# Half-size products for one more batch, and another order of the last stores, in an attention and mixer kernel

## The chip, the cores and the metric

The kernel runs on one core of a Trainium2 chip. The metric is the time of one execution on the device in microseconds (us), and less is better. Several runs of one kernel are summed up by their median. A profile is one further execution, taken by the hardware profiler: it gives the start and the length of each instruction on each engine. The engines are TensorE (PE in the profile; its weight loads are listed apart as PEld), VectorE (DVE), ScalarE (ACT), GpSimd (POOL) and SyncE (SP), which here only issues DMAs. Each engine works through its own queue in order, and an instruction that has to wait holds up all that stand behind it on that engine.

## The reference: what is computed

Four batches, each of 8 heads, 768 positions and a head width of 64, go through an attention with a window of 128 and 4 sink positions. Its output (768 x 512 for each batch) goes through a mixer: one product pair over the positions (768 to 256 to 768), and then one over the channels (512 to 1536 to 512), each with a ReLU between.

```python
scores = scale * np.matmul(q, k.transpose(0, 1, 3, 2))
rel = pos[:, None] - pos[None, :]
keep = (pos[None, :] < n_sink) | ((rel >= 0) & (rel < window))
a = softmax(np.where(keep, scores, -1e9))        # exp over its sum + 1e-9
x = np.matmul(a, v)                              # heads side by side: 4 x 768 x 512
h = np.maximum(x.transpose(0, 2, 1) @ w_tok1, 0.0) @ w_tok2
u = x + h.transpose(0, 2, 1)
h2 = np.maximum(u @ w_ch1, 0.0) @ w_ch2          # w_ch1 512 x 1536, w_ch2 1536 x 512
out = u + h2
```

The change lies in the last product, `relu(u @ w_ch1) @ w_ch2`, and in how its result is added to u and stored. Here the batches are called first to fourth; in the code they are b = 0 to 3.

## The kernel before

All is bf16 on TensorE with fp32 sums in PSUM. PSUM has eight banks: four single ones, `ps_ga` to `ps_gd`, which everything but the scores uses in turn, and two pairs, `ps_sa` and `ps_sb`, for the scores. Once the last score has been computed, the pairs serve the products too.

The work is written as small tasks: a function that issues instructions, an engine or a choice of engines, an estimated duration, the tasks that it depends on, and a priority. `Plan.order` plays these tasks through with the estimated durations, picks for each engine the ready task of lowest priority, chooses the PSUM bank, and so fixes the order in which each engine's instructions are issued. At the end the priorities are overwritten by the table `RANK`, one number for each task in the order of their making. So the order on all engines is decided before the run; on the chip, only the waits between engines are left. The order is one interleaving of the attention of a later batch with the mixer of an earlier one.

The stages of the mixer, for batch b:

- `make_tok`: the product pair over positions (the lines L999 and L1041 of the profile), then `u = h + x` on DVE (L1047) and a DMA transpose of u into `uT` (L1053), issued from SP.
- `ch1(half, ft)` in `make_channel` (L1100): 24 groups of four matmuls over 384 columns, one for each half of the positions and each of 12 channel tiles. Each fills one bank, and a ReLU on ACT (L1058) or DVE (L1060) moves it to `v1`, which holds `[channel, position]`.
- the product with `w_ch2`. The first two batches do it by `ch2` (L1249): six position tiles, each 12 matmuls over 512 columns into one bank, in three parts of four. The result is added to u by one DVE instruction of 512 columns (L1265) and stored by one DMA of 256 KB (L1280).
- The third and the fourth batch do it by `products` (L1151): v1 is split into quarters a11, a12, a21, a22 by position and channel, w_ch2 likewise, and seven products of half size take the place of eight. `sub` (L1126) makes four sums of quarters on DVE, in three chunks of 768 elements each: S3 = a11 - a21, S1 = a21 + a22, S2 = S1 - a11, S4 = a12 - S2. They lie in the tiles that the profile names x_ba or x_bb (S3), q32a (S1), k32a (S2) and v (S4). The tiles q32a and k32a are the landing place of the q and k loads of even groups of heads, so a sum has to wait until POOL has cast what was loaded there. `make_weight_sums` (L1076) makes the four sums of quarters of w_ch2 once, as eight DVE or POOL instructions.

A product is one task: six matmuls of 256 columns. `pair(i)` combines the products of the position tiles i and i + 3 into their output tiles by `read` (L1182, L1184, and L1179 for the one that adds one product to both halves of a tile), always on DVE. The sequence `TURNS`, a list of product number and pair, gives the first order of the products, before `RANK`. The products 1, 6 and 7 of a pair follow each other in one bank, with a read after each; products 5 and 3 share another.

In the last pair of the last batch, before the change, the first output tile stores its left half, the second tile its whole width, and product 3 closes: in two pieces of 128 columns, each read and stored by itself (L1227), the very last from ACT's queue.

Of the kernel before, what the change touches and what calls it, by code (L numbers as in the profile page):

```python
# [44 lines left out]
ACT_MORE = 0.05  # L45
LATE_CAST = [None, None, ('ACT', 'DVE'), ('ACT', 'DVE'), ('ACT', 'DVE')]
MASK_ENG = {0: ('DVE',), 1: ('POOL',), 2: ('POOL',), 3: ('POOL',), 4: ('POOL', 'DVE'), 5: ('DVE',), 6: ('POOL', 'DVE'), 7: ('POOL',)}
KS_ENG = {0: ('POOL', 'ACT'), 1: ('ACT', 'DVE'), 2: ('ACT', 'DVE'), 3: ('POOL', 'DVE'), 4: ('ACT', 'DVE'), 5: ('ACT', 'DVE'), 6: ('ACT',
    'DVE'), 7: ('ACT', 'DVE')}
# [7 lines left out]
RANK = [0, 0, 27, 389, 474, 75, 75, 0, 0, 50, 50, 110, 130, 410, 150, 1105, 74, 556, 294, 761, 901, 1005, 1169, 1384, 1534, 2175, 2603,  # L57
    3040, 3395, 2965, 3530, 100, 170, 520, 570, 170, 1751, 1345, 1564, 1613, 1352, 2093, 3275, 3682, 350, 249, 319, 310, 319, 461, 424,
    691, 663, -90, -209, 525, 525, 1010, 704, 830, 510, 587, 609, 844, 971, 1062, 1305, 1485, 406, 731, -132, 783, 711, 1347, 963, 1080,
    504, 1220, 1285, 1341, 1431, 1332, 1606, 1681, 2305, 2886, 2489, 1812, 1948, 2034, 1968, 1353, 1432, 2116, 2138, 2764, 2198, 2143,  # L60
    2171, 2307, 831, 963, 909, 1267, 142, 1053, 1318, 1371, 1354, 1867, 1194, 1489, 1520, 1191, 1717, 1365, 1590, 1782, 1644, 1468,
    1884, 1751, 2006, 1825, 1636, 1968, 2208, 1979, 2328, 1501, 1921, 1829, 2331, 1924, 1941, 2257, 2251, 2726, 2394, 2424, 2250, 2394,
    2507, 2285, 2344, 2470, 2240, 2466, 2385, 2482, 2421, 3095, 2898, 2330, 2692, 2563, 2706, 2589, 2651, 2773, 3162, 2922, 3261, 3351,
    2965, 2635, 2984, 3084, 2930, 2521, 3370, 3380, 3033, 3404, 3353, 3213, 3889, 3385, 3694, 3110, 3509, 3495, 3414, 3640, 3729, 5285,
    3724, 3740, 3659, 4045, 3754, 3810, 3479, 3735, 4001, 4476, 3986, 4082, 4091, 4307, 4123, 3669, 4098, 3974, 4055, 4201, 4100, 4586,
    4475, 4501, 4510, 5226, 4622, 4848, 4627, 4623, 4542, 4898, 4917, 5099, 5128, 5244, 5246, 5391, 5293, 5496, 6289, 5519, 5924, 5949,
    6243, 6486, 6575, 6044, 6899, 6655, 6790, 6910, 7063, 7112, 7523, 7555, 7715, 7836, 7169, 7737, 8153, 8173, 8261, 8289, 8553, 8707,
    8835, 8971, 4021, 3787, 4465, 3215, 3969, 4124, 4116, 4190, 3897, 3672, 3524, 3908, 4037, 3989, 4113, 4126, 4506, 4505, 4683, 4692,
    4922, 4362, 5079, 5243, 3683, 5355, 4388, 4009, 5244, 5700, 4483, 5261, 5079, 5363, 5605, 5991, 5620, 5761, 5654, 5741, 5798, 5854,
    4927, 5262, 4827, 5342, 4431, 5086, 4375, 5649, 5329, 5427, 5403, 5237, 5068, 5398, 5523, 5596, 6036, 5743, 5970, 6049, 6037, 6377,  # L70
    6393, 6398, 5703, 5515, 6148, 6326, 6581, 7097, 6834, 6797, 6772, 6806, 6785, 6856, 6779, 6868, 7043, 7106, 7077, 6436, 6036, 6062,
    6041, 6128, 7285, 7091, 7170, 7257, 7349, 7487, 7291, 7402, 8027, 7886, 7664, 7781, 8011, 7874, 7938, 8166, 7967, 8067, 8371, 7940,
    8067, 8376, 8866, 8952, 8301, 9017, 9075, 9161, 9140, 9226, 9217, 9303, 9272, 9368, 9347, 9493, 9500, 9556, 9730, 9786, 10365, 9521,
    9931, 9087, 9966, 10052, 10290, 10396, 10805, 10441, 10420, 10386, 10365, 10451, 10430, 10621, 10792, 10980, 11056, 10636, 10722,
    10787, 10853, 10799, 10965, 10944, 11400, 11209, 11280, 11101, 11419, 11581, 11095, 11241, 11306, 11392, 11458, 11484, 11523, 11539,
    11688, 11360, 11943, 12070, 12114, 11614, 11787, 12109, 12127, 12171, 12076, 12278, 11777, 12564, 12721, 12132, 12473, 12721, 12916,
    13080, 5334, 5349, 5339, 5389, 5449, 5853, 6011, 6070, 5819, 6001, 6186, 6000, 6528, 6663, 6069, 6324, 6602, 7140, 6884, 6904, 6246,
    7229, 6864, 7416, 7434, 7523, 6923, 7024, 7390, 6820, 6953, 7038, 7459, 7746, 7260, 7298, 7822, 8185, 8434, 8235, 8187, 8285, 8242,
    8305, 8217, 8325, 8221, 8405, 5489, 5604, 5679, 5784, 5929, 6024, 6699, 6204, 7103, 6553, 6845, 7306, 7444, 6963, 7432, 8330, 8090,
    8390, 7903, 8534, 8610, 8748, 8847, 8996, 9096, 9123, 9213, 8520, 8803, 8864, 9022, 9229, 9365, 8605, 9273, 9412, 9487, 9436, 9537,  # L80
    9565, 9591, 9570, 9041, 9695, 9811, 8452, 8599, 8548, 8634, 9800, 9916, 9835, 9952, 10031, 10095, 10236, 10074, 10155, 10361, 10747,
    10244, 10506, 10190, 10304, 10641, 10203, 10334, 10736, 10247, 10414, 10801, 7900, 8157, 8490, 8538, 8496, 8573, 8763, 8841, 13190,
    12686, 12808, 12902, 12953, 12429, 13017, 13103, 13074, 13199, 13159, 13245, 13224, 13310, 13289, 13305, 13412, 13498, 13581, 13587,
    13646, 13732, 13842, 13928, 13907, 13993, 14061, 14137, 14086, 14172, 14151, 14237, 14332, 14418, 14671, 15357, 14819, 14805, 14804,
    14890, 14967, 15053, 15367, 15473, 15563, 15329, 15628, 15714, 14187, 14252, 14314, 14096, 15292, 14740, 15396, 15492, 15444, 15559,
    15620, 15718, 14903, 14689, 14968, 15055, 15042, 15816, 15748, 15849, 15177, 15263, 15879, 15965, 15944, 16031, 16089, 16039, 15034,
    15120, 15111, 15203, 15813, 15932, 16141, 16227, 16793, 16879, 16401, 16927, 16924, 17046, 17135, 17035, 15301, 15577, 16206, 16293,
    16616, 16710, 16727, 16814, 16662, 16748, 16858, 16986, 16989, 17079, 17185, 17085, 9191, 9286, 9381, 9566, 9621, 9726, 9721, 9926,
    8307, 10121, 10191, 10475, 10827, 10846, 10956, 12423, 12363, 12425, 12478, 12598, 12695, 12752, 12811, 12968, 13048, 13064, 13455,
    12554, 12655, 12858, 12976, 13246, 13314, 13082, 13149, 13054, 13402, 13377, 13452, 13477, 13543, 13512, 13433, 13547, 13933, 9801,  # L90
    10046, 9541, 10636, 10791, 10786, 11271, 11396, 9511, 11103, 12533, 12703, 13011, 12591, 13099, 13964, 13970, 13972, 14072, 14202,
    14253, 14484, 14605, 14632, 14722, 14832, 14179, 14291, 14427, 15039, 14701, 14987, 14869, 14901, 15032, 15156, 15055, 15126, 15176,
    15232, 15211, 15282, 15246, 15332, 13711, 13798, 13777, 13863, 15282, 15589, 15498, 15434, 15093, 15677, 15831, 15776, 15517, 15956,
    15779, 15877, 16041, 15523, 15936, 16206, 15866, 15996, 16331, 15909, 16056, 16456, 16988, 17426, 17053, 17491, 17718, 17556, 17183,
    17621, 17248, 17686, 17313, 17901, 17228, 17816, 17443, 17881, 17508, 17946, 17573, 18011, 17638, 18076, 17703, 18131, 17848, 18206,
    17833, 18271, 17898, 18336, 17963, 18401, 18114, 18466, 18266, 18531, 18417, 18596, 18442, 18811, 18633, 18988, 18785, 19053, 19236,
    19118, 19001, 19183, 18394, 18469, 18551, 18613, 18684, 18749, 18830, 18881, 20076, 19241, 19322, 19403, 18640, 18767, 18715, 18848,
    19424, 19517, 19358, 19451, 19293, 19484, 19620, 19707, 19555, 19641, 19689, 19781, 18771, 18929, 18836, 18976, 19489, 19576, 19686,
    19772, 20013, 20101, 19751, 20148, 20144, 20268, 20332, 20222, 19082, 19289, 19227, 19370, 19882, 19969, 19948, 20034, 19817, 19903,
    20079, 20208, 19417, 19988, 20282, 20210, 20301, 20382, 20243, 20321, 20355]  # L100
STRASSEN = {2, 3}
EARLY_P = {2: 0, 3: 4}
TURNS = '10 20 11 21 60 50 61 70 30 40 51 12 22 71 42 62 52 41 72 31 32'
S_CHUNK = 2
S_ENG = {1: ('DVE',), 2: ('DVE',), 3: ('DVE',)}
T_ENG = ('POOL', 'DVE')

SEM = 0.05
PE_TAIL = 0.16


def flat_list(x):
    return [z for y in x for z in (flat_list(y) if isinstance(y, (list, tuple)) else [y])]


# [220 lines left out]
def kernel(  # L336
# [742 lines left out]
    def make_channel(b):  # L1079
# [7 lines left out]
        if b == 0 and RES_DMA:  # L1087
            for x in range(2):
                def f(t, x=x):
                    nc.sync.dma_start_transpose(out=u.rearrange("p t d -> p (t d)").rearrange("p (n d) -> p n d", d=P)[:, ts(x, 2 * NT)],  # L1090
                                                in_=uT_[:, 2 * x:2 * x + 2].rearrange("p c s -> p (c s)"))
                M.back.append(add("SP", 1.3, f, [M.turn, L["v3"], L["k3"]], prio=BIAS.get("back", 0) + 5, dma=2.7, run=0.42))
        seq = iter(range(base, base + 200))

        def ch1(half, ft):
            slot = Slot()

# [245 lines left out]
    with tc.manual_schedule():  # L1343
# [3 lines left out]

        for t, r in zip(plan.tasks, RANK):
            t.prio = r
# [38 lines left out]
```

## Time and profile before

| what | value |
|---|---|
| runs (us) | 203.08, 202.29, 203.17, 203.13; median 203.11 |
| profiled execution | 202.05 us, of which the span from the first to the last instruction is 200.3 us |
| mean granted TensorE clock | 0.998 |
| busy in the span: PE | 192.7 us (96%) |
| busy in the span: DVE, ACT, POOL | 125.3 us (63%), 107.2 us (54%), 66.7 us (33%) |
| HBM read, written | 26.77 MB, 6.29 MB |
| PE waits above 0.1 us after the first 20 us | one, of 0.4 us |

The profiled execution is 0.24 us below the fastest and 1.06 us below the median of the four runs. Its own sums are therefore made within its 200.3 us span, and only the difference is carried over to the median.

The columns of a group row are: line, engine, operation, output <- inputs, size, number of instructions; then the busy time, the mean time of one in ns, and the idle time before them. In a row of the timeline they are: start, length, engine, line, operation, and in brackets how long the engine had been idle and what ended it. Matmuls overlap in their pipeline, so the length of one matmul in a group row (380 ns for 512 columns) is longer than the step from one to the next; the chain of waits gives the steps.

### The profile page before, as it was taken

The numbers are of one execution on the slowest core, as the hardware profiler recorded it, in microseconds if no ns is written. First come the engines' busy times: TensorE is split into PE (matmuls) and PEld (weight loads), VectorE is DVE, ScalarE is ACT, GpSimd is POOL, SyncE is SP. The second block draws the span as 40 slices with busy tenths as digits, with TensorE's granted clock in tenths as the row PEclk, the third lists the DMA queues.
The fourth block names the chain that finished last, engine by engine and source line by source line (L and its number), as shares of the span: only waits on it lengthen the run. The fifth ranks groups of instructions, "written<-read, shape, count | busy, mean of one in ns | idle before, by whom it ended". The sixth has DMA issues, their size and how long they took to land.

```text
span 200.3 us, 4471 instructions
## 1 busy us (share of the span) xinstructions
PE 192.7 (96%) x1742; PEld 123.8 (62%) x1742; DVE 125.3 (63%) x303; ACT 107.2 (54%) x188; POOL 66.7 (33%) x110
## 2 busy tenths in 40 slices
PE   7799999999999999999999999999999999999992
PEld 2444876656665655657645544576587687658881
DVE  4689870747655779978262112885699964056782
ACT  2799377788978852496614203787813003773000
POOL 8994422047795762200614011004870000000000
PEclk9999999999999999999999999999999999999999
DMA  5999999999399999699998599900000256100034
GB/s 171 357 229 181 209 206 334 225 266 199 94 285 186 235 188 130 169 150 185 202 197 149 115 203 236 273 12 3 0 0 3 47 165 207 57 0 3 26 146 142
DMA packets 74870, 30.98 MB, mean 155 GB/s; under 512 B 63650, under 2 KB 71202, under 8 KB 74850
## 3 DMA queue, kind: packets, MB, share of 16 engines
q1 hardware_dynamic: 43938, 18.85, 42.4%
q0 software_dynamic: 29680, 10.22, 41.7%
q10 hardware_dynamic: 1232, 1.64, 2.4%
q8 instruction: 13, 0.21, 0.5%
q14 instruction: 7, 0.06, 0.1%
HBM read 26.77 MB, written 6.29 MB: 165 GB/s over the span
## 4 chain that ended last, share of the span: by engine, by line
PE 82%; DMA 11%; DVE 2%; POOL 1%; ACTq 0%; issue 0%; DVEq 0%
PE ps_ga L1100 9%; DMA w_tok<-in_moe_w_tok_dram 8%; PE ps_gc L1100 8%; PE ps_gd L1100 8%; PE ps_gb L1100 7%; PE ps_gb L1249 5%; PE ps_gd L1249 4%; PE ps_gc L1249 4%; DMA k32a<-in_k_dram 3%; PE ps_ga L1151 3%; PE ps_gb L1151 3%; PE ps_ga L1249 3%; PE ps_sa L825 2%; PE ps_sa L1151 2%; PE ps_gc L1151 2%; PE ps_gd L1151 2%
## 5 line engine op out<-in xcount | busy, mean ns | idle before, releaser
L1100 PEld LDWEIGHTS <-w_ch 128*128 128x128 bf16 x384 | 36.7, 98 | 24.4 <-issue 1.4
L1058 ACT ACTIVATE v<-ps_gc 128x384 bf16<-128x384 f32 x22 | 10.8, 492 | 25.7 <-PE ps_gc L1100 25.5
L1249 PEld LDWEIGHTS <-v 128*128 128x128 bf16 x144 | 13.4, 98 | 14.0 <-issue 0.6
L1151 PEld LDWEIGHTS <-v 128*128 128x128 bf16 x150 | 14.1, 98 | 2.3
L1058 ACT ACTIVATE v<-ps_ga 128x384 bf16<-128x384 f32 x21 | 10.4, 494 | 6.8 <-PE ps_ga L1100 6.5
L1058 ACT ACTIVATE v<-ps_gd 128x384 bf16<-128x384 f32 x17 | 8.3, 490 | 8.2 <-PE ps_gd L1100 7.3
L1249 PE MATMUL ps_gb<-w_ch,v 128*128 128x512 bf16 x48 | 12.3, 380 | 0.0
L1100 PE MATMUL ps_ga<-uTa,w_ch 128*128 128x384 bf16 x56 | 11.4, 326 | 0.0
L1100 PE MATMUL ps_gd<-uTa,w_ch 128*128 128x384 bf16 x52 | 10.6, 326 | 0.4 <-DVE x_bb L955 0.4
L479 POOL DMA_DIRECT2D vab<-in_v_dram x4 | 5.7, 1437 | 14.9 <-PE ps_gd L937 12.4
L1100 PE MATMUL ps_gc<-uTb,w_ch 128*128 128x384 bf16 x52 | 10.6, 326 | 0.0
L999 PEld LDWEIGHTS <-w_tok 128*128 128x128 bf16 x96 | 9.1, 98 | 2.0 <-issue 0.4
L1058 ACT ACTIVATE v<-ps_gb 128x384 bf16<-128x384 f32 x17 | 8.4, 492 | 3.6 <-PE ps_gb L1100 3.4
L1100 PE MATMUL ps_ga<-uTb,w_ch 128*128 128x384 bf16 x48 | 9.8, 326 | 0.0
L1249 PE MATMUL ps_gd<-w_ch,v 128*128 128x512 bf16 x36 | 9.2, 379 | 0.0
L1249 PE MATMUL ps_gc<-w_ch,v 128*128 128x512 bf16 x36 | 9.2, 379 | 0.0
L1100 PE MATMUL ps_gb<-uTb,w_ch 128*128 128x384 bf16 x44 | 9.0, 327 | 0.0
L1100 PE MATMUL ps_gc<-uTa,w_ch 128*128 128x384 bf16 x44 | 9.0, 326 | 0.0
L436 POOL CAST kbb<-k32b 128x768 bf16<-128x768 f32 x5 | 4.3, 874 | 13.4 <-DMA k32b<-in_k_dram 13.4
L479 POOL DMA_DIRECT2D vaa<-in_v_dram x4 | 6.0, 1490 | 7.8 <-PE ps_ga L937 6.5
L1100 PE MATMUL ps_gb<-uTa,w_ch 128*128 128x384 bf16 x40 | 8.1, 327 | 0.0
L1100 PE MATMUL ps_gd<-uTb,w_ch 128*128 128x384 bf16 x40 | 8.1, 326 | 0.0
(399 smaller groups left out, 506.3 us busy)
## 6 DMA issues: line engine op xcount, KB each, us to landing
q32a<-in_q_dram SPq DMA_DIRECT2D x4, 384.0 KB, 4.4
vaa<-in_v_dram POOLq DMA_DIRECT2D x4, 384.0 KB, 11.8
vab<-in_v_dram POOLq DMA_DIRECT2D x4, 384.0 KB, 11.9
w_ch<-in_moe_w_ch_dram POOLq DMA_DIRECT2D x3, 512.0 KB, 15.0
w_ch<-in_moe_w_ch_dram POOLq DMA_DIRECT2D x2, 768.0 KB, 19.6
q32b<-in_q_dram SPq DMA_DIRECT2D x8, 192.0 KB, 7.6
k32b<-in_k_dram SPq DMA_DIRECT2D x8, 192.0 KB, 3.5
out_dram<-oa SPq DMA_DIRECT2D x4, 256.0 KB, 4.8
```

The source lines that it names most:

```text
L436: on(t).tensor_copy(out=o, in_=i)
L479: t = add(eng, hold, lambda t: e.dma_start(out=o, in_=i), deps, prio=prio, dma=work, run=run)
L825: nc.tensor.matmul(half(slot, i)[:, at:at + w].rearrange("p (c q) -> p c q", q=P), qkT(kT, g, j)[ds(64 * i, 64), kt], qkT(qT, g, j)[ds(64 ...
L999: nc.tensor.matmul(flat(slot)[:, 0:GH * D], w_tok1[:, n, ts(tt, P)], x[:, n, ds(a * GH * D, GH * D)], start=(n == 0), stop=(n == NT - 1))
L1058: nc.scalar.activation(o, i, AF.Relu)
L1100: nc.tensor.matmul(flat(slot)[:, 0:HS], w_ch1[:, c, ts(ft, P)], uT_[:, c, ds(half * HS, HS)], start=(c == 0), stop=(c == NC - 1))
L1151: nc.tensor.matmul(flat(slot)[:, 0:cw], A[n][0][:, x, ts(i, P)], W[n][:, x, ds(c0, cw)], start=(first and x == 0), stop=(x == NH - 1), ski ...
L1249: nc.tensor.matmul(flat(slot)[:, 0:cw], v1[:, ft, ts(st, P)], w_ch2[:, ft, ds(c0, cw)], start=(ft == 0), stop=(ft == NF - 1 and (b > 0 or ...
```

## The change

1. `STRASSEN` takes in b = 1: the second batch's last product goes by seven half products instead of by `ch2`. The sums of w_ch2 are made before it, that is with the first batch.
2. In the last pair of the last batch, product 3 comes before product 4, and product 4 is the one done in two pieces. The residual of the second tile's left half is copied into its output tile ahead of time by a new copy on ACT or POOL (`keep`), and the wide read of product 7 adds to that. Both tiles are stored by quarters or halves: left and right half of the first, right half of the second, and its left half in two pieces.
3. The engines allowed for the masks of group 6 (`MASK_ENG`, now POOL alone) and for the small copies of sink keys (`KS_ENG`) change, and ACT's surcharge in the planner goes (`ACT_MORE`).
4. `RANK` is a new table, so the order on every engine is another one. `seq2` and the addition of 15000 are part of how priorities are numbered.

```diff
-ACT_MORE = 0.05
+ACT_MORE = 0
-MASK_ENG = {0: ('DVE',), ... 4: ('POOL', 'DVE'), 5: ('DVE',), 6: ('POOL', 'DVE'), 7: ('POOL',)}
-KS_ENG = {0: ('POOL', 'ACT'), 1: ('ACT', 'DVE'), 2: ('ACT', 'DVE'), 3: ('POOL', 'DVE'), 4: ('ACT', 'DVE'), ...
+MASK_ENG = {0: ('DVE',), ... 4: ('POOL', 'DVE'), 5: ('DVE',), 6: ('POOL',), 7: ('POOL',)}
+KS_ENG = {0: ('ACT',), 1: ('POOL', 'ACT', 'DVE'), 2: ('POOL', 'ACT', 'DVE'), 3: ('POOL', 'ACT', 'DVE'), 4: ('ACT', 'DVE'), ...
-RANK = [0, 0, 27, 389, 474, 75, 75, 0, 0, 50, ...
+RANK = [0, 12, 27, 429, 556, 90, 80, 0, 0, 50, ...
-STRASSEN = {2, 3}
-EARLY_P = {2: 0, 3: 4}
-TURNS = '10 20 11 21 60 50 61 70 30 40 51 12 22 71 42 62 52 41 72 31 32'
+STRASSEN = {1, 2, 3}
+EARLY_P = {1: 0, 2: 0, 3: 4}
+TURNS = '10 20 11 21 60 50 61 40 70 51 41 30 12 71 22 62 52 31 72 32 42'
...
+        seq2 = iter(range(base + 30000, base + 30200)) if b == B - 1 else seq
...
                 d = Slot()
-                p4 = product(i, 4, d, True, True, [])
-                r4 = read(o2, d, 0, DH, [p4, w2], op=ALU.subtract, res=s2, frees=True)
                 p7 = product(i, 7, a, False, True, [r6])
-                r7 = read(o2, a, 0, DM, [p7, r4, r5], frees=True, wide=True)
-                order += [(4, p4), (7, p7)]
+                order.append((7, p7))
                 if not end:
+                    p4 = product(i, 4, d, True, True, [])
+                    r4 = read(o2, d, 0, DH, [p4, w2], op=ALU.subtract, res=s2, frees=True)
+                    r7 = read(o2, a, 0, DM, [p7, r4, r5], frees=True, wide=True)
+                    order.append((4, p4))
...
                 else:
                     store(s1, o1, 0, DH, [r2])
                     r5b = read(o1, bb, DH, DH, [p5, r6], frees=True)
-                    store(s2, o2, 0, DM, [r7])
+                    p3 = product(i, 3, d, True, True, [])
+                    r3 = read(o1, d, DH, DH, [p3, r5b], frees=True)
+                    store(s1, o1, DH, DH, [r3])
+                    order.append((3, p3))
+
+                    def keep(t):
+                        copy(t, o2[:, 0:DH], u[:, s2, 0:DH])
+                    r0 = add(("ACT", "POOL"), {"ACT": act(DH, True), "POOL": 0.4}, keep, w2, prio=6)
+                    r7 = read(o2, a, 0, DM, [p7, r0, r5], frees=True, wide=True)
+                    store(s2, o2, DH, DH, [r7])
                     for x in range(2):
                         e = Slot()
-                        p = product(i, 3, e, True, True, [], c0=128 * x, cw=128)
-                        r = read(o1, e, DH + 128 * x, 128, [p, r5b], frees=True)
-                        store(s1, o1, DH + 128 * x, 128, [r], x == 1)
-                        order.append((3, p))
+                        p = product(i, 4, e, True, True, [], c0=128 * x, cw=128)
+                        r = read(o2, e, 128 * x, 128, [p, r7], op=ALU.subtract, frees=True)
+                        store(s2, o2, 128 * x, 128, [r], x == 1)
+                        order.append((4, p))
...
-                    t.prio = M.early_prio + 0.01 * n if n < EARLY_P[b] else next(seq)
+                    t.prio = M.early_prio + 0.01 * n if n < EARLY_P[b] else next(seq2)
...
+        for t in plan.tasks[len(RANK):] if RANK else []:
+            if t.prio < 1000 and t.eng != ("SP",):
+                t.prio += 15000
```

## The prediction

> **What bounds the kernel now.** I read the busy table first, then the busy time by stretches, then PE's waits and the chain of waits, and last the timeline at the places that the change touches.
>
> ```profile
> span 200.3 us, 4471 instructions
> PE 192.7 (96%) x1742; PEld 123.8 (62%) x1742; DVE 125.3 (63%) x303; ACT 107.2 (54%) x188; POOL 66.7 (33%) x110
> ```
>
> ```profile
> 100.00:110.00 10.00, 10.00 (x55) 5.18 (x54) 4.47 (x7) 3.60 (x8) 3.20 (x4) 1.00 1.23 171
> 110.00:120.00 10.00, 10.00 (x51) 4.80 (x49) 1.40 (x3) 1.47 (x3) 0.83 (x1) 1.00 0.76 155
> ...
> 150.00:160.00 10.00, 9.56 (x89) 7.18 (x86) 9.61 (x24) 2.03 (x5) 0.00 (x0) 1.00 0.09 19
> ```
>
> ```profile
> PE ps_gd L1100 <- DVE x_bb L955: 0.4, 1, 0.4
> ```
>
> ```profile
> 102.45 0.86 PE ps_gb L1249 x4
> ...
> 145.89 0.66 PE ps_ga L1151 x6
> ```
>
> In the stretches the columns are length, then PE, PEld, DVE, ACT, POOL, the clock, DMA. PE is full from 20 to 195 us at full clock, but for 0.44 us near 150 us, where it waits for a busy DVE. So PE work removed in between shortens the run one for one, as long as the others keep up. In the second batch's last product (100 to 124 us) DVE is almost idle; in the third batch's (150 to 160 us) DVE is full: that is what seven products cost DVE when attention work runs beside them. The chain gives the steps: four matmuls of 512 columns 0.86 us (215.6 ns each), six of 256 columns 0.656 us (109.3 ns each).
>
> **PE work of the second batch.** Removed: 18 groups of four, 18 x 0.862 = 15.5 us. Added: 21 products, 21 x 0.656 = 13.8 us. All other PE instructions stay in number. Saved: 1.7 us, all on the path. Here a rule speaks against the change: the Trainium skill, TensorE: Matmul & The Clock Gate, Back-to-back issue gap, gives for streams of weight load and matmul a sustained 81 ns at 128 columns and 131 ns at 512. On a straight line between (an estimate from that page), 256 columns take 98 ns: 126 x 98 = 12.3 us against 72 x 131 = 9.4 us, a loss of 2.9 us. The rows above are from this kernel's own streams of pairs, with weight loads of 98 ns under each matmul, and a half product costs half. I take the trace.
>
> **DVE work of the second batch.** Removed: six reads of 512 columns, one each 0.60 us. Added: 18 reads of 256 columns at a step of 0.34 us and three wide ones at 0.60, 7.9 us; twelve sums at 0.47 us (0.60 where one needs the one before it), about 6.2 us. So DVE gets 10.5 us more, in a stretch that has over 14 us free. DVE hides as a sum; what counts is the place where a product needs the last chunk of sums:
>
> ```profile
> 185.85 0.81 PE L1100 MATMUL ps_sb<-uTb,w_ch 128*128 128x384 bf16 x4
> ...
> 186.70 0.49 ACT L1058 ACTIVATE v<-ps_sb 128x384 bf16<-128x384 f32 x1 [1.41 <-PE ps_sb L1100]
> ...
> 187.22 0.56 DVE L1126 TENSOR_TENSOR q32a<-v 128x768 bf16<-128x768 bf16 x1 [0.75 <-ACT v L1058]
> ...
> 188.03 0.55 DVE L1126 TENSOR_TENSOR k32a<-q32a,v 128x768 bf16<-128x768 bf16 x1
> ...
> 188.46 0.82 PE L1151 MATMUL ps_sa<-sums_w,q32a 128*128 128x256 bf16 x6
> ...
> 189.12 0.82 PE L1151 MATMUL ps_gd<-sums_w,k32a 128*128 128x256 bf16 x6
> ```
>
> In the fourth batch, from the start of the last ReLU (186.70) to the last S2 (188.58) it is 1.9 us, with one read between. PE covers it with three products on quarter a22 and one on S1, and does not wait. I followed the same in the changed kernel's instruction order, which is known without times. In the second batch PE has only two products between the last ch1 and the first product on S2, and four of that product's six matmuls need only earlier chunks: 2 x 0.656 + 4 x 0.109 = 1.75 us after ch1's end. DVE's queue: ReLU starts 0.16 after that end, S1 0.52 later, then a read (it stands between, start +0.47), then S2 from about +1.5 to +2.05, behind which the matmul starts. PE waits 0.3 to 0.4 us. Before it, ch1 groups use one bank twice with a single product between (0.656 us), where wait, ReLU and release take 0.16 + 0.49 + 0.05 = 0.7: about 0.05 us, three times. I take 0.5 us together. Lower bound 0.2 (the waits cover each other), upper 1.2 (one more read and one more sum in front).
>
> What is queued behind the waiting S2 on DVE: the read of product 4, S4, and the reads that free ps_ga and ps_gd. Adding up their steps (0.34, 0.60, 0.47) from there, each bank is released at least 0.1 us before PE takes it again (rotation 1.97 us), up to the third batch's ch1. S1's and S2's tiles are also freed by POOL's casts of group 6; of these the last counts:
>
> ```profile
> 106.55 0.83 POOL L436 CAST kba<-k32a 128x768 bf16<-128x768 f32 x1 [2.81 <-DMA k32a<-in_k_dram]
> ```
>
> On SP's queue its load moves behind one q32b load (SP takes 0.8 to 2.6 us for each here), on POOL's the cast moves behind another cast (0.83). So it ends near 109 to 111, S2's last chunk starts at 112.7: hidden, with 2 us to spare. SP's u transposes, too, are no later: one k32b load has gone from in front of them. The key transposes of the fourth batch lie before the sixth u transpose now, hence earlier.
>
> **Sums of w_ch2.** The eight DVE instructions (0.55 us, 4.4 in all) move from 80 to 92 us to 36 to 48 us: no more, but DVE has 9.7 of 15 us busy there. The first waits for the second half of w_ch2: issued at 20.64, landing after 19.0 to 20.2 us, so at about 40.8. Behind it and two more sums stands the copy of q's transposes to SBUF (0.96 us): done at about 44.0, needed by the scores at 44.55. The copies and ReLUs behind come 0.3 to 1 us before PE needs them. I take 0 (an upper bound is the rival below).
>
> **Third batch.** Here DVE is the bound before. Its order now has three reads and an S3 between the normalisations that free PE's banks. Adding the steps: the fourth normalisation ends 0.15 us too late for ps_gb, the fifth 0.4 too late for ps_sb, 0.55 in all against 0.44 before. Added 0.1 us, between -0.4 (order better than I add) and +0.7. For POOL beside it there is a rule: GPSIMD Engine Reference, Specifications, of the same skill says that GpSimd's SBUF interface is shared with DVE instructions of two SBUF inputs, which the sums are. The trace agrees in kind:
>
> ```profile
> 141.33 0.66 DVE L1126 TENSOR_TENSOR q32a<-v 128x768 bf16<-128x768 bf16 x1
> ...
> 141.54 0.71 POOL L902 TENSOR_SCALAR_AFFINE_SELECT pTc<-pTc 128x256 bf16<-128x256 bf16 x1
> ```
>
> The sum takes 0.66 in place of 0.55, the POOL instruction 0.71 in place of 0.40. By the rule all twelve new sums are at risk, by the trace only those beside POOL work: five casts in the second batch. So 2 x 0.15 us, in the upper bounds above. Group 6's masks go from DVE to POOL (9 us in 124 to 134 us, POOL idle before but for one cast); adding up, the first is ready 1 us before its product. Taken as 0.
>
> **The end.**
>
> ```profile
> 195.01 0.82 PE L1151 MATMUL ps_gc<-sums_w,x_bb 128*128 128x256 bf16 x6
> ...
> 195.87 0.69 DVE L1179 TENSOR_TENSOR of<-ps_gc,of 128x512 f32<-128x512 f32 x1 [0.22 <-PE ps_gc L1151]
> 196.00 0.50 PE L1151 MATMUL ps_gd<-w_ch,v 128*128 128x128 bf16 x6
> ...
> 196.68 0.28 DVE L1184 TENSOR_TENSOR oe<-ps_gd,oe 128x128 f32<-128x128 f32 x1
> ```
>
> The wide read holds DVE over PE's end (196.50), so the last read starts 0.18 us after it, and the 256 KB store is issued 0.4 us before the last 64 KB. Now a whole product lies between product 7 and the two pieces: the wide read ends in its shadow, the last read starts 0.04 us after PE's end, 0.14 us gained, and 128 KB less is queued in front of the last store (up to 0.2 us more, or nothing, as the last store lands 1.9 us after its issue in any case). The copy of the residual (POOL, idle by then) and the extra store on SP cost nothing: SP has 0.33 us each and all but two are issued before PE ends. I take -0.2 (bounds 0 and -0.4).
>
> **Sum.** -1.7 + 0.5 + 0.1 - 0.2 = -1.3 us: in the profiled execution 202.05 to about 200.7, span 199. The profiled one stood 1.06 below the median, so for the median 203.11 - 1.3 = 201.8 us.
>
> **The rivals.**
>
> A, slower: DVE falls behind in 36 to 48 us. Work there becomes 9.7 + 4.4 - 0.9 (the small key copies go to ACT and POOL, a copy to ACT) = 13.2 of 15 us, in order, and its first sum waits for a DMA. From a landing at 41.3 on, each us goes to PE, which stands full in this stretch; from about 43 on, or with 1.3 us of DVE backlog otherwise, the gain is gone. With a landing or backlog 2.5 us later than I add: 203.11 - 1.3 + 2.5 = 204.3. For it: DMA is busy to nine tenths there, and DVE holds copies that scores wait for. Against: in the profile before that landing is no later than 41, and 80 to 92 us gets the same work off DVE.
>
> B, nothing to tell: PE's new waits in the second and third batch reach their upper bounds (1.2 + 0.7 in place of 0.6) and the start costs some tenths through its new order: 203.0. For it: DVE's 9.61 of 10 in the third batch.
>
> C, more: the third batch's wait goes (-0.5) and the end gains 0.4: 201.1. That the change doesn't do what it says is excluded: the instruction order has 126 half matmuls in the second batch.
>
> **How the numbers follow.** Forecast with C 0.67 (its own range 201.0 to 202.5), B 0.14, A and its like 0.19. A measurement of this kernel tells about 0.3%, 0.6 us, from no change. Faster 0.67, same 0.14, slower 0.19. The range 200.9 to 203.9 leaves out some 0.06 below (C with all lower bounds) and 0.11 above (A at its full price).
>
> **What would show it.** Right: PE busy falls by about 1.7 us, L1249's 72 matmuls gone; one wait of PE for DVE's k32a sum near 113 us of 0.2 to 0.8 us; the wait near 150 us still there, 0.3 to 0.8; the last read within 0.1 us of PE's end. Wrong: PE waits for DVE between 40 and 50 us or for w_ch there; PE waits for POOL's masks near 130 us; a mean step of half products above 0.115 us; a last product group followed by more than 3.6 us to the end.

## The result, and the profile after

| | before | after |
|---|---|---|
| median of the runs (us) | 203.08 (63 runs) | 201.72 (44 runs) |
| lowest | 202.03 | 200.57 |
| ratio, 95% interval | | 0.9938 [0.9926, 0.995] |
| profiled execution, its span | 202.05, 200.3 | 201.79, 200.1 |

The change takes 1.36 us off the median; 201.8 was predicted. The ratio leaves out 11 slow runs of the kernel before, all above 205 us; the other 52 average 202.76 us and the 44 runs of the changed kernel 201.51 us, 1.26 us less. But the two profiled executions differ by 0.26 us only. Whoever compares just these two profiles finds PE ending at the same time (196.50 and 196.49 us) and would say that the change to the products brought nothing. Most of what follows explains that contradiction.

The page of the changed kernel, its span and its busy times:

```profile
span 200.1 us, 4614 instructions
PE 191.9 (96%) x1796; PEld 129.2 (65%) x1796; DVE 135.5 (68%) x313; ACT 107.6 (54%) x190; POOL 76.3 (38%) x132
```

54 matmuls more (72 out, 126 in), and DVE has 10.2 us more work (10.5 were counted). The same stretches as before (length, then busy PE, PEld, DVE, ACT, POOL, clock, DMA):

```profile
100.00:110.00 10.00, 10.00 (x66) 6.18 (x64) 7.92 (x14) 4.41 (x9) 3.64 (x4) 1.00 1.44 153
110.00:120.00 10.00, 9.86 (x84) 7.95 (x83) 7.74 (x18) 1.68 (x4) 0.83 (x1) 1.00 0.96 184
...
150.00:160.00 10.00, 9.79 (x93) 7.46 (x90) 9.37 (x22) 2.10 (x5) 0.00 (x0) 1.00 0.13 16
```

DVE fills the second batch's stretch to three quarters (4.47 and 1.40 us before), and PE stays full but for 0.14 us. Of PE's waits after 20 us the list names three (what waited, for whom, us, times, longest):

```profile
PE ps_gd L935 <- POOL pTd L901: 0.5, 1, 0.5
PE ps_gd L1025 <- DMA w_tok<-in_moe_w_tok_dram: 0.4, 1, 0.4
...
PE ps_sb L1103 <- DVE x_bb L957: 0.2, 1, 0.2
```

The last is the third batch's (0.4 before). The first is new, and in no step of the prediction. The second, at the landing of w_tok near 26.7 us, is 0.2 us in the next profile of the same kernel. The end, in the timeline (start, length, engine, line, operation):

```profile
195.25 0.69 DVE L1182 TENSOR_TENSOR of<-ps_gb,of 128x512 f32<-128x512 f32 x1 [0.28 <-issue]
...
195.99 0.50 PE L1154 MATMUL ps_gd<-sums_w,v 128*128 128x128 bf16 x6
...
196.52 0.29 DVE L1185 TENSOR_TENSOR of<-of,ps_gd 128x128 f32<-128x128 f32 x1
...
196.89 0.37 ACTq L1240 DMA_DIRECT2D out_dram<-of  x1
```

The wide read (195.25 to 195.94) is over before PE's end at 196.49; the last read starts 0.03 us after it, and not 0.18. From PE's end to the span's: 3.6 us, before 3.8.

**Where PE's time went.** For each matmul I take the time from its start to the start of the next, less the step of its shape (0.1093 us for 256 columns, 0.2157 for 512, and so on), and add these up by stretches. The sum of the steps falls from 183.86 to 182.10 us; what PE loses besides moves like this:

| stretch of the span (us) | before | after | difference |
|---|---|---|---|
| 0 to 66 (with w_tok's landing near 26.7, the sums of w_ch2) | 8.39 | 8.48 | +0.09 |
| 66 to 76 | 0.38 | 1.25 | +0.87 |
| 76 to 100 | 0.65 | 0.76 | +0.11 |
| 100 to 124 (second batch's products) | 0.21 | 0.69 | +0.48 |
| 124 to 156 (third batch) | 1.54 | 1.73 | +0.19 |
| 156 to PE's end | 0.00 | 0.00 | 0.00 |

So the products did save 1.76 us of PE's work, and in this execution 0.87 us of it were lost again in ten microseconds in which nothing of the products had changed.

### The profile page after: what moved, and what is told of

Same layout as the page of the kernel before. It is cut to its first block, busy times and chain, and to the rows that moved or that the text cites. A ratio compares the mean times of both kernels' runs of the same rounds, so it can differ in the third digit from the quotient of the medians.

```text
span 200.1 us, 4614 instructions
## 1 busy us (share of the span) xinstructions
PE 191.9 (96%) x1796; PEld 129.2 (65%) x1796; DVE 135.5 (68%) x313; ACT 107.6 (54%) x190; POOL 76.3 (38%) x132
## 4 chain that ended last, share of the span: by engine, by line
PE 74%; DMA 15%; DVE 3%; POOL 2%; SPq 2%; issue 1%; ACT 0%; ACTq 0%; DVEq 0%; POOLq 0%
PE ps_gb L1103 9%; DMA w_tok<-in_moe_w_tok_dram 8%; PE ps_gc L1103 8%; PE ps_gd L1103 7%; PE ps_ga L1103 6%; PE ps_gc L1154 5%; PE ps_ga L1154 5%; DMA q32b<-in_q_dram 4%; PE ps_gd L1154 4%; DMA k32a<-in_k_dram 3%; PE ps_gb L1154 3%; SPq L481 2%; PE ps_sa L1154 2%; PE ps_sa L827 2%; PE ps_gc L1262 1%; PE ps_sb L827 1%
## 5 line engine op out<-in xcount | busy, mean ns | idle before, releaser
L1060 ACT ACTIVATE v<-ps_gb 128x384 bf16<-128x384 f32 x26 | 12.8, 491 | 26.9 <-PE ps_gb L1103 26.5
L1103 PE MATMUL ps_gb<-uTb,w_ch 128*128 128x384 bf16 x72 | 14.6, 326 | 0.0
L1129 DVE TENSOR_TENSOR x_bb<-v 128x768 bf16<-128x768 bf16 x6 | 3.4, 559 | 13.1 <-ACT v L1060 13.1
L1060 ACT ACTIVATE v<-ps_ga 128x384 bf16<-128x384 f32 x16 | 7.9, 492 | 3.9 <-PE ps_ga L1103 3.8
L1060 ACT ACTIVATE v<-ps_gc 128x384 bf16<-128x384 f32 x16 | 7.8, 490 | 2.8 <-PE ps_gc L1103 2.3
L871 ACT ACTIVATE pTa<-ps_sa 128x1024 bf16<-128x1024 f32 (+1 forms) x5 | 4.9, 976 | 6.6 <-PE ps_sa L827 6.6
L1154 PE MATMUL ps_gc<-w_ch,v 128*128 128x256 bf16 x60 | 8.2, 273 | 0.0
L871 ACT ACTIVATE pTc<-ps_sb 128x1024 bf16<-128x1024 f32 (+1 forms) x6 | 5.8, 960 | 3.2 <-PE ps_sb L827 3.1
L1103 PE MATMUL ps_ga<-uTb,w_ch 128*128 128x384 bf16 x36 | 7.3, 327 | 0.0
L1103 PE MATMUL ps_ga<-uTa,w_ch 128*128 128x384 bf16 x36 | 7.3, 326 | 0.0
```

The source lines that it names most:

```text
L871: nc.scalar.activation(dst[:, :, 512 * u:512 * u + w], ps_s[slot.at[1]][:, :, 0:w], AF.Exp, scale=scale)
L1060: nc.scalar.activation(o, i, AF.Relu)
L1103: nc.tensor.matmul(flat(slot)[:, 0:HS], w_ch1[:, c, ts(ft, P)], uT_[:, c, ds(half * HS, HS)], start=(c == 0), stop=(c == NC - 1))
L1129: on(t).tensor_tensor(out=sums_a[n][:, r], in0=in0, in1=in1, op=op)
L1154: nc.tensor.matmul(flat(slot)[:, 0:cw], A[n][0][:, x, ts(i, P)], W[n][:, x, ds(c0, cw)], start=(first and x == 0), stop=(x == NH - 1), ski ...
```

## The experiments

Steps are moved in the finished order with a small helper, so that the instructions of one engine change places and nothing else does:

```
def ahead(n, m):            # put task n ahead of task m
    at = {t.n: x for x, t in enumerate(todo)}
    t = todo.pop(at[n])
    todo.insert(at[m], t)
```

### Both kernels once more

No edit. The changed kernel:

> The changed kernel once more, to see how its waits move from one execution to the next. Theory 1 (the gain is PE work of the second batch, and PE's wait of 0.55 us for a POOL mask near 70 us, which the first profile shows, is part of this kernel's own order): the wait is there again at 0.4 to 0.7 us, and the time is 201.7 us (201.3 to 202.0). Rival (the wait is the mark of one unlucky execution, its DMA load landing late by chance): no wait above 0.2 us for a mask in this profile, and a span nearer to 199.2 us.

Measured: 201.70 us (200.59 to 202.54). The profiled execution took 201.05 us, and no wait for a mask is in its list (by the steps 0.17 and 0.15 us are lost there, 0.71 and 0.15 in the first profile). Matmul by matmul, it runs 0.20 us ahead of the first profile from 30 us to 68.5 us and 0.74 ahead at 70 us, and keeps just these 0.74 to PE's end. So 0.54 us of the difference of two executions of one program arise at one spot. In the first profile the spot looks like this:

```profile
64.74 0.82 POOL L438 CAST qbb<-q32b 128x768 bf16<-128x768 f32 x1
67.41 0.83 POOL L438 CAST qbb<-q32b 128x768 bf16<-128x768 f32 x1 [1.86 <-DMA q32b<-in_q_dram]
68.19 0.70 POOL L901 TENSOR_SCALAR_AFFINE_SELECT pTd<-pTd 128x384 bf16<-128x384 bf16 x1
...
69.22 0.69 POOL L901 TENSOR_SCALAR_AFFINE_SELECT pTd<-pTd 128x384 bf16<-128x384 bf16 x1
...
69.97 0.20 PE L935 MATMUL ps_gd<-vab,pTd 128*128 128x65 bf16 x1 [0.55 <-POOL pTd L901]
```

POOL stands 1.86 us before a cast whose load has not landed, and behind the cast wait the four last masks, which PE needs. In the kernel before, all eight masks stood ahead of that cast (64.36 to 67.7 us); its last two steps there:

```profile
67.13 0.58 POOL L902 TENSOR_SCALAR_AFFINE_SELECT pTd<-pTd 128x256 bf16<-128x256 bf16 x1
67.67 0.82 POOL L436 CAST qbb<-q32b 128x768 bf16<-128x768 f32 x1
```

The load landed at 67.41 here, and the cast could start at 66.85 in the second profile: half a microsecond decides. In three more profiles with this order on POOL (two of them in the experiments "One step moved on DVE" and "A longer warming", where the cast starts at 66.20 and 65.78 us) no such wait is left at all. So the rival had the fact right, that the wait comes and goes, and the theory the place and the cause: a new order on POOL that leans on a load. Why the load lands at different times stays open.

The kernel before:

> The kernel before once more, to see whether its own time moves in the same place. The changed kernel's two profiles (201.79 and 201.05 us) differ by 0.74 us, and all of it arises at one spot, near 70 us, where POOL's cast waits for a load of q32b. Theory (the loads of the third batch's first group land late in both kernels, and the time of a run says how late): a profile of 202.8 to 203.3 us would show 0.6 to 1.1 us of PE waits between 55 and 75 us which the first profile (202.05 us) did not have; a profile near 202.1 us none. Rival: a profile near 203.1 us shows its extra time spread over the run, at its start or behind PE's last matmul.

Measured: 203.16 us, an execution of the upper of two groups of runs (see below), and the rival was right: no wait at 55 to 75 us; the extra 1.1 us are all made between 6 and 11 us. First this execution, then the one of 202.05 us:

```profile
6.01 0.82 PE L746 MATMUL ps_ga<-ident,qba 128*128 128x128 bf16 x6 [1.16 <-ACT qba L434]
...
7.27 1.06 PE L808 MATMUL ps_sa<-mneg,ident 128*128 128x512 bf16 x2
```

```profile
6.14 0.51 PE L746 MATMUL ps_ga<-ident,qba 128*128 128x128 bf16 x6 [1.29 <-ACT qba L434]
...
6.82 0.60 PE L808 MATMUL ps_sa<-mneg,ident 128*128 128x512 bf16 x2
```

The same matmuls, at half the rate: two of 512 columns step by 0.85 us (7.27 to the next at 8.12) in place of 0.43. PE loses 1.9 us up to 9 us and gets 0.8 of them back where it waits anyway. The profile's clock column shows 1.00 in both, so it does not tell:

```profile
6.00:8.00 2.00, 1.99 (x14) 1.57 (x15) 0.95 (x4) 0.98 (x3) 1.83 (x2) 1.00 1.13 377
```

### A longer warming

```diff
-N_IDLE = 8
+N_IDLE = 11
```

> The changed kernel with eleven instead of eight warming matmuls at the start (N_IDLE 11), so that PE is busy until its first transpose at about 6.1 us. Runs of both kernels fall into two groups about 1 us apart; the profile of the kernel before at 203.16 us has the matmuls between 6.3 and 10 us at half their rate (0.10 us for 128 columns in place of 0.056), the one at 202.05 us has not. Theory (the idle stretch from 4.9 to 6.1 us decides by chance whether PE is still slow after it; each group is one case): the upper group goes, the spread of the undisturbed runs shrinks from 1.5 to 0.8 us or less (what is left is the wait for POOL near 70 us), and the median falls to 200.6 to 201.4 us. Rival (slow or fast is decided at the start of the program, whatever PE does in between): two groups as before, median 201.5 to 202.0 us, later by the 0.2 us that the extra matmuls hold up the first transpose.

> The kernel before with eleven warming matmuls. Theory: only its lower group stays, 202.1 us in the median (201.9 to 202.4), and the changed kernel with eleven is 0.7 to 1.5 us faster than this one, by whether the wait near 70 us shows. Rival (as for the changed kernel with eleven): two groups, median 203.1 us.

Measured: the kernel before 202.20 us (eleven runs, 202.00 to 202.32, and one of 206.15), the changed one 200.79 us (five runs, 200.72 to 200.85, and one of 201.44, which has no profile). In the kernel before the upper group is gone: without the edit 26 of its 63 runs lay at 202.03 to 202.66 us, 23 at 202.89 to 203.49 and 14 from 204 us on. In the changed kernel, where 28 of 44 runs lay at 201.51 to 201.97, none of the six does. In it PE now works through to its first transposes:

```profile
1.26 4.87 PE L1359 MATMUL ps_ga<-warm 128*128 128x512 bf16 x11 [1.26 <-DVE warm L442]
6.08 0.60 PE L748 MATMUL ps_ga<-ident,qba 128*128 128x128 bf16 x6
```

This agrees in kind with the Trainium skill, TensorE: Matmul & The Clock Gate, What's actually happening: PE runs at half rate until it has been busy for some 3.4 us, and how long that takes varies from run to run, because the window in which activity is counted runs freely. The page lets the moment vary by 0.5 us to either side; here it varies by more. With eleven warming matmuls PE comes to full rate 5.1 us after the first of them in the profile above (6.34 us), 3.0 us after it in the last experiment below (4.2 us), and 6.0 us after it in the kernel before, whose first transposes still go at half rate:

```profile
6.00 0.82 PE L746 MATMUL ps_ga<-ident,qba 128*128 128x128 bf16 x6
6.62 0.80 PE L746 MATMUL ps_gb<-ident,kba 128*128 128x128 bf16 x6
7.25 0.59 PE L808 MATMUL ps_sa<-mneg,ident 128*128 128x512 bf16 x2
```

Eight warming matmuls last 3.6 us here and are followed by 1.2 us of idleness; then PE is at full rate from its first transpose on, or, in the two profiles with a slow start, only from 10.0 and 10.6 us on. Eleven leave the moment to chance too, but in all three profiles with them it came by 7.25 us. With like starts, then, the two kernels are 202.20 and 200.79 us: 1.41 us apart, a ratio of 0.9930. The profile of the changed kernel has no wait at 70 us there, so that wait is hardly in this figure.

### The end alone

The kernel before, with the changed `pair` and ranks of its own for the last pair; the copy is left to POOL, and product 4 waits for product 3 in the order. All else is as before (in the profile PE's work runs at a constant 0.12 us behind that of the kernel before, from 30 to 190 us). The cut shows it against the changed kernel, without the tables that are those of the kernel before:

```diff
-STRASSEN = {1, 2, 3}
+STRASSEN = {2, 3}
-                    r0 = add(("ACT", "POOL"), {"ACT": act(DH, True), "POOL": 0.4}, keep, w2, prio=6)
+                    r0 = add(("POOL",), {"POOL": 0.4}, keep, w2, prio=6)
-                        p = product(i, 4, e, True, True, [], c0=128 * x, cw=128)
+                        p = product(i, 4, e, True, True, [p3], c0=128 * x, cw=128)
```

> The kernel before with the new end alone: in the last pair product 3 before product 4, product 4 in two pieces, the residual copied ahead by POOL, quarters stored one by one; the second batch still goes by ch2, and all other orders are those of before. Theory 1 (the prediction's term for the end): 0.2 us less than before, 0 to 0.4, from PE's last matmul to the end of the span 3.6 us in place of 3.8. Rival (the end is a larger part of the gain of 1.36 us, through fewer bytes in front of the last store): 0.7 us or more less than before.

Measured: 202.94 us against 203.07, ratio 0.9997 [0.9967, 1.0028], which by itself tells nothing. By groups: the lower one lies at 201.71 to 202.08 us (before 202.05 to 202.29), the upper at 202.78 to 203.21 (before 202.92 to 203.22). PE's last matmul ends at 196.62 us of a span of 200.1: 3.5 us, before 3.8. The medians of the two groups differ by 0.3 and 0.2 us. Theory 1 stands, 0.2 to 0.3 us; the rival's 0.7 is out. No run takes the half products of the second batch without the new order, so what the other points of the change are worth by themselves is known only from the sums of steps.

### One step moved on POOL

```
ahead(325, 537)     # the last masks of pTd before the second cast of q32b
```

> The changed kernel with one step moved on POOL's queue alone: the last four masks of pTd (group 3) come before the second cast of q32b to qbb, which waits for a load that lands at 67.4 us, and no longer behind it. Theory 1 (the cast holds up the masks, and PE waits for them near 70 us for 0.55 us and loses another 0.14 at the next step): the wait goes, and the kernel takes 0.5 to 0.8 us less than the changed kernel, about 201.0 us. Rival (PE's time there is given back at the next wait, for the q transposes or for a bank): the wait goes at 70 us but another of like size comes before 85 us, time as the changed kernel, 201.7 us.

Measured: 201.53 us (200.55 to 202.54), ratio to before 0.9943 [0.9919, 0.9967]; the changed kernel beside it had 0.9942. In the profile (201.41 us) the wait at 70 us is gone; PE gains 0.71 and 0.15 us there on the first profile of the changed kernel. But it had lost 0.34 and 0.37 us at 62.6 and 63.6 us, waiting for ACT and DVE, which in their turn had waited for the loads of q32a and k32a (k32a's landed at 61.38 us, in the other profiles so far at 60.5 to 61.2). These stand ahead of the moved step, and no order of POOL has changed there: another execution, another late load. Neither side of the expectation is shown by the times: the start's chance and the loads of 55 to 67 us hide 0.5 us in twelve runs. Nor does this one profile prove the cause, as the wait is missing from others with the old order too; that rests on the rows of the first profile, where the masks follow the late cast without a gap.

### One step moved on DVE

```
ahead(430, 465)     # S2's third chunk before the read of ps_gb
```

The wait that was predicted for the second batch, in the first profile of the changed kernel:

```profile
113.54 0.42 DVE L1187 TENSOR_TENSOR oe<-ps_gb,u_sbb 128x256 f32<-128x256 f32 x1
...
113.74 1.13 PE L1154 MATMUL ps_ga<-sums_w,k32a 128*128 128x256 bf16 x6
...
113.87 0.55 DVE L1129 TENSOR_TENSOR k32a<-q32a,v 128x768 bf16<-128x768 bf16 x1
```

The product takes 1.13 us in place of 0.82: 0.31 us of waiting inside it, for the sum that a read precedes.

> The changed kernel with one step moved on DVE's queue alone: the third chunk of S2 in the second batch comes before the read of ps_gb into oe, and no longer behind it. Theory 1 (the prediction's: PE waits 0.3 us near 114.5 us for that chunk, because the read of 0.34 us stands ahead of it): the wait shrinks to under 0.05 us and the time falls by 0.2 to 0.35 us against the changed kernel. Rival (the read that is now later frees ps_gb too late, or the next product is what PE waits for): PE waits 0.2 to 0.4 us at a product between 115 and 118 us, and the time stays as the changed kernel's within 0.1 us.

Measured: 201.57 us (200.44 to 201.66) against 201.70, within the spread; by the steps PE gains 0.15 us at this product, and nothing comes in its place. So half of the wait was the read's. The other half belongs to the chain ReLU, S1, S2 itself: S1 ended at 112.73 and S2 at 113.37 with nothing between, and PE wanted it at 113.28. The theory is right in kind and twice too large.

### PE work taken out of the second batch

Each of the second batch's three products number 4 leaves out three of its six matmuls, and so half of its sum.

```diff
-for x in range(NH):
+for x in range(3 if b == 1 and n == 4 else NH):
```

> The changed kernel without nine matmuls of 256 columns in the second batch: each of the three products number 4 runs over three of its six channel tiles only, so half of its sum is left out. All orders and all work of the other engines stay. Theory (PE bounds, and PE work removed in the second batch comes out at the end one for one): 9 x 0.109 = 0.98 us less than the changed kernel, 200.7 us. Rival (DVE's reads and sums bound the stretch from 108 to 122 us, and PE would wait for them instead): 0.5 us or less saved, with new PE waits for DVE between 114 and 122 us or in the third batch.

Measured: 201.44 us (200.60 to 201.89). The rival was right. From 100 us to PE's end the profile gains 0.33 us on the changed kernel's, not 0.98:

```profile
113.44 0.60 PE L1155 MATMUL ps_ga<-sums_w,k32a 128*128 128x256 bf16 x4
114.52 0.39 PE L1155 MATMUL ps_ga<-sums_w,k32a 128*128 128x256 bf16 x2 [0.47 <-DVE k32a L1129]
...
122.63 0.81 PE L1155 MATMUL ps_gc<-w_ch,v 128*128 128x256 bf16 x6 [0.19 <-DVE of L1188]
```

Of three pieces of 0.33 us the first only makes PE wait longer for S2 (0.47 us in place of 0.14 in this column), the second makes it wait for the read that frees ps_gc, the third arrives at the end. This profile had a slow start. It shows what such a start does to the wait at 70 us: PE is 0.91 us behind the first profile of the changed kernel up to 69 us and 0.03 us behind from 71 us on, because the load has landed before PE comes (POOL's two casts follow each other without a wait). "PE is full" was good for the step that the change took, and not for the next one: after it, the second batch is bound by DVE's chain in two places.

### All orders mended

Four orders are mended, in five moves:

```
ahead(325, 537); ahead(430, 465)        # as above
ahead(640, 649)                         # third batch: a ReLU before the first S2
ahead(793, 652); ahead(795, 652)        # third batch: two normalisations before S1 and S2
```

The reason for the third line, in the first profile of the changed kernel:

```profile
143.59 1.15 POOL L882 TENSOR_TENSOR pTd<-pTd,mask 128x512 bf16<-128x512 bf16 x1
143.85 1.31 DVE L1129 TENSOR_TENSOR k32a<-q32a,v 128x768 bf16<-128x768 bf16 x1
```

Beside POOL's mask the sum takes 1.31 us, not 0.55; the ReLU queued behind it is late, and PE loses 0.27 us at 145.7. The last line alone:

> The changed kernel with two steps moved on DVE's queue alone: in the third batch the last two normalisations (x_bb from ps_sb and from ps_ga) come before the sums S1 and S2 of the second chunk, and no longer behind them. Theory (the prediction's: what PE waits for near 151 us is DVE's order, not DVE's sum of work): the 0.37 us near 151.9 us go, and nothing comes in their place before 156 us; 0.3 us less than the changed kernel, 201.4 us. Rival (DVE is full there, so the sums that are now later make PE wait for the product on q32a at 154.5 us): the wait moves there, and the time stays within 0.1 us of the changed kernel's.

Measured: 201.45 us (200.35 to 201.69), 0.25 us less than 201.70, as the theory has it, but within the spread. Its profile is of an execution of 498.5 us and can't decide it. All four:

> The changed kernel with four orders mended together: on POOL the last four masks of group 3 before the second cast of q32b, on DVE the third chunk of S2 of the second batch before the read of ps_gb, in the third batch the ReLU from ps_gd before the first S2 (which takes 1.31 us there beside POOL's mask, in place of 0.55) and the last two normalisations before two sums. If the gains of the single moves add up (0 to 0.7 by where the load lands, 0.15, 0.27 and 0.37 us): 0.8 to 1.4 us less than the changed kernel, 200.3 to 200.9 us in the median, faster than both kernels. Rival (each move's later step is the next to be waited for): 0.4 us or less, 201.3 us or more.

Measured: 200.71 us (200.07 to 201.17), ratio to before 0.9877 [0.9842, 0.9913]. Of PE's waits only these are left after 10 us:

```profile
PE ps_gd L1025 <- DMA w_tok<-in_moe_w_tok_dram: 0.6, 1, 0.6
PE ps_sa L814 <- ACT pTc L871: 0.3, 1, 0.3
```

Against the second profile of the changed kernel PE gains 0.3 us at the masks, 0.15 at S2's product and 0.27 at the ReLU. At the normalisations it gains 0.37 and loses 0.14 again at the next product (151.14 us): something came in their place after all, and 0.1 us more goes in small gaps. From 112 us to PE's end 0.54 us arrive of the 0.79 that the three moves on DVE were to bring. So the moves add up in the main, and the time is in the expected range. Then with the longer warming:

> The four mended orders and eleven warming matmuls together. Theory: only the lower group of the runs with the four mended orders (200.07 to 200.36 us) stays, 200.2 us in the median, 200.0 to 200.5. Rival (warming only helps where the wait near 70 us is not moved): 200.7 us or more.

Measured: 200.17 us (199.88 to 200.82), ratio to before 0.9848 [0.9803, 0.9894]: 3.0 us below the kernel before, 1.5 below the changed one. The one run at 200.82 us is the profiled one; its stretch from 50 to 66 us loses 2.23 us in place of about 1.5, with a wait for DVE's copy of k (kTa), the same sight as in the profile with the masks moved. Both have the moved masks, but so has the profile of all four orders, which does not show it. The loads before 67 us are what is left of the spread, as far as the profiles tell.

## Why the prediction was right, and where it was not

- **PE work of the second batch**, -1.7 us: -1.76, by the steps of the trace. The estimate weighed against it (98 ns for 256 columns, a loss of 2.9 us) does not hold here: the new products step by 0.656 us (112.43, 113.08, 113.74), 109 ns each.
- The sign that was named for it, PE busy less by 1.7 us, was wrong: it fell by 0.8. A matmul of 256 columns is 0.27 us long and steps by 0.11, so a wait of up to 0.16 us lies under the one before it and counts as busy. The wait list is short by as much: 0.55 in the list is 0.71 in the steps.
- **Waits in the second batch**, +0.5 us: +0.48, of which 0.30 at S2's third chunk (0.3 to 0.4 predicted) and 0.09 twice at ch1's bank (0.05 three times predicted).
- **Sums of w_ch2**, 0: the first starts at 41.12 us, when w_ch2's second half has landed (40.8 predicted, PE in danger from 41.3), and PE has no wait between 30 and 60 us. Rival A did not come, with 0.2 us to spare.
- **Third batch**, +0.1 us: +0.19, and not for the reason given. The two waits at the normalisations are as forecast: 0.16 and 0.37 us (0.15 and 0.4). But the 0.44 us before, with which they were compared, are a figure of the wait list; by the steps it was 0.61, so these two alone are 0.08 us less. What was added is 0.27 us at the ReLU behind a slow sum (145.7 us). The term for POOL beside DVE's sums was too small: 2 x 0.15 us were allowed for, in the upper bounds alone, and single sums took 0.63 (108.71 us) and 0.76 us (143.85 us) more. Masks of group 6 on POOL: no wait of PE near 130 us.
- **The end**, -0.2 us: 3.8 to 3.6 us in the changed kernel, 3.8 to 3.5 with the end alone.
- **What was missing**: the new order on POOL at 64 to 70 us, which cost 0.87 us in the first profile, 0.32 in the second and nothing in three others. POOL's queue was looked at near 106 and 130 us, and not here, where no part of the change lies. With it the forecast for a fast start would have been up to 0.9 us higher.
- **The profile's distance from the median**, 1.06 us, was carried over as a constant. In the kernel before it is the difference of PE's two kinds of start. In the changed kernel it is not a constant: a fast start lies 0.65 us below the median in the second profile and 0.07 us above it in the first, and a slow start hides the wait at 70 us. So the forecast of 200.7 us for the profiled execution is near the lowest 11 of 44 runs (200.57 to 200.97) and was missed by both profiles (201.05 and 201.79), while the median came within 0.1 us.
- **Luck.** That closeness is in part luck. The missing wait and the distance that shrinks have opposite signs. And the median of the kernel before lies in the upper of two groups only through its 14 runs from 204 us on: without them it is 202.37 us, and the difference 0.65. The averages given with the result (1.26 us) and the two kernels with the longer warming (1.41 us) do not hang on this, and they bear out the 1.3 us. So sign, path and the size of the main terms were right.
- In the rivals, B's terms add up to 203.1 us before the start's tenths, not to 203.0; nothing rests on it.

## What to carry to other kernels

When two profiles of the same program differ, line their matmuls up by number before comparing kernels: here the start moves a run by 1.1 us and one late load by up to 0.7, nearly as much as the change itself. A new order has to be read on all queues and not only where the edit is: an instruction that waits for a load holds up all behind it, and nothing urgent belongs there. Work taken off the bounding engine pays only until the next chain is as long: here 1.76 us less brought 0.48 us of new waits in the same stretch, and of a further 0.98 only 0.33 arrived.

## What the runs showed of the hardware that I had not expected

- With 1.2 us of idleness after 3.6 us of warming matmuls, PE starts at full or at half rate by chance, by the two groups of times about half the runs each in the kernel before; half rate then lasts until 10.0 or 10.6 us (two profiles) and costs 1.1 us in the end. The clock column of the profile shows 1.00 throughout. With warming matmuls up to the first transpose, full rate came 3.0 to 6.0 us after the first matmul (three profiles).
- A DVE sum of two bf16 tiles of 768 elements takes 0.55 us alone, and 0.66 to 1.31 us beside POOL instructions; what a single overlap costs was 0.11 to 0.76 us.
- The loads of the third batch's first group land up to 0.9 us apart in executions of the same order (k32a at 60.53 and 61.38 us), and the load of q32b that held up the masks 1.2 us apart in three with a fast start (66.20, 66.85 and 67.41 us): enough to turn a queue order from harmless to 0.7 us.
